# RWKV-style attention into a max-out MLP: token-major sums onto a bonus in PSUM, with every engine's order written out

## The chip, the core and the metric

The kernel runs on one core of one Trainium2 chip. The metric is the device time of one execution in microseconds (us); the value of a kernel is the median of its runs.

## The reference

For each batch and head a state of 48 x 48 is carried along 768 tokens; the output of a token sees the state before it and a bonus for the token itself. The result is then the input of a feed-forward block with the larger of two linear maps as its nonlinearity.

```python
B, H, S, D = 4, 8, 768, 48
for t in range(S):
    cur = einsum('bhd,bhe->bhde', u * k[t], v[t])
    y[t] = einsum('bhd,bhde->bhe', r[t], state + cur)
    state = w[t][..., None] * state + einsum('bhd,bhe->bhde', k[t], v[t])
x = y.transpose(0, 2, 1, 3).reshape(3072, 384)
out = maximum(x @ w1, x @ w2) @ w_out          # w1, w2: 384 x 1024, w_out: 1024 x 384
```

The kernel uses max(a, b) = (a + b + |a - b|) / 2: the hidden layer holds |x (w1 - w2)|, and x (w1 + w2) w_out / 2 is one product with a matrix wc that is made once.

## The kernel before

The tokens are cut into chunks of 128 (C), six for each sequence. A **unit** is one chunk of two sequences (NB = 2, called blocks b below), and there are twelve, chunk after chunk, the two pairs of sequences alternating. Units 10 and 11 are the last chunk and update no state.

For a unit, `attention` loads w, k, r and v, takes the logarithm of w (lw), sums it over the tokens of the chunk with a product by an upper triangle (`ex_p`, fp32, on PE), and takes exponentials: Aex (decay up to the token before), and Ainv (its inverse with the token itself) from incl = ex_p + lw. r and k are scaled by them into rp and kp, whose heads are padded to 64 columns. PE transposes both (`tp`), DVE copies them out (`rkT`), PE forms the scores of the eight heads (`mt_p`), and DVE masks them with the triangle (`MTm`). The output is summed in `y_p` **feature-major**: rows are features and columns tokens, three banks-worth of 128 features. Three products with the identity put in the bonus (vd, v times the row sums dg of r u k, made by DVE over L185, L186, L188 and L190); six put in the state's share; ten put in the values' share. Because a head's 48 features cross the borders of 128, `vz` and `sz` hold heads between zeros and are read through windows, so that a head can appear in two products. ACT copies `y_p` to xT, already in the shape that the feed-forward wants. `kv_p` collects k v for the state; DVE adds it to `sf` in two halves and scales it with Wx, the chunk's decay, which comes from the last row of incl through DRAM (`row`, `Wt`); POOL casts the state into `sz`.

`feed_forward` of the unit before follows: 24 products of the hidden layer (`g_p`) with ACT's absolute value (`gT`), then for each block three products with wc and eight with w_out (`o_p`), a copy (`osb`) and a store. `prep_weights` makes w1 - w2 (wd_sb), w1 + w2 (ws_sb), its transpose (wsT_sb) and wc after unit 0's attention.

Nothing in the code of before fixes the order on an engine: the framework's scheduler merges unit i's attention and unit i-1's feed-forward, within the limits of buffers. All loads and stores are issued from SP, one queue in order.

## Time and profile before

| what | us |
|---|---|
| median of 3 runs (193.05, 194.99, 195.09) | 194.99 |
| the profiled execution | 193.31 |
| its span, first to last instruction | 191.5 |
| busy in it: PE / DVE / ACT / POOL | 163.8 / 145.3 / 83.3 / 41.3 |
| idle of POOL before L248, waiting for DVE | 74.0 |
| idle of ACT before L228, waiting for PE | 43.9 |
| idle of DVE before L160, waiting for ACT's Aex | 21.3 |

PE is the tensor engine's products and PEld its weight loads, DVE the vector engine, ACT the scalar engine, POOL GpSimd and SP the queue that issues DMAs. A row of a group has line, engine, operation, written tile <- read tiles, shape and count, then busy time and the mean ns of one, then the idle time ahead of it and what ended that. A row of a timeline has start, length and what ran; "x8" joins eight instructions in a row.

### The profile page before, as it was taken

How to read it: one execution, taken by the hardware profiler on the slowest of the kernel's cores; microseconds unless marked ns; L12 is line 12 of the kernel's file. 1: busy time of each engine (PE TensorE's matmuls, PEld its weight loads, DVE VectorE, ACT ScalarE, POOL GpSimd, SP SyncE). 2: the span in 40 equal slices, each digit the busy share in tenths (PEclk: the TensorE clock that was granted, in tenths of full speed). 3: DMA queues.
4: the chain of work that ended last, by engine and by line, in shares of the span. 5: the costliest groups of instructions: out<-in, count | busy, mean ns of one | idle time of the engine just before them, and what ended most of it. 6: DMA issues, size and time to landing. Idle time of an engine off the chain costs nothing.

```text
span 191.5 us, 3963 instructions
## 1 busy us (share of the span) xinstructions
PE 163.8 (86%) x1624; PEld 111.7 (58%) x1624; DVE 145.3 (76%) x184; ACT 83.3 (43%) x158; POOL 41.3 (22%) x52
## 2 busy tenths in 40 slices
PE   0615875389999989999999999999999999999992
PEld 0203642236766667666766767667667666666761
DVE  0169998975747988999899799798997997937300
ACT  3120221313565365383573644734736357344351
POOL 8993020005021032041300310213103112100000
PEclk9999999999999999999999999999999999999999
DMA  6999998992029779498495894975948769110112
GB/s 140 219 331 382 196 281 221 199 166 47 3 92 233 132 154 169 106 215 147 98 234 88 184 182 92 236 138 122 213 84 203 133 135 195 38 44 5 41 41 82
DMA packets 112614, 28.82 MB, mean 150 GB/s; under 512 B 107594, under 2 KB 111818, under 8 KB 112596
## 3 DMA queue, kind: packets, MB, share of 16 engines
q1 hardware_dynamic: 112596, 28.58, 68.7%
q8 instruction: 12, 0.20, 0.4%
q14 instruction: 6, 0.05, 0.1%
HBM read 23.82 MB, written 4.75 MB: 149 GB/s over the span
## 4 chain that ended last, share of the span: by engine, by line
PE 48%; DVE 25%; issue 8%; ACT 8%; DMA 5%; SPq 3%; POOL 1%; ACTq 0%; DVEq 0%; POOLq 0%
PE o_p L272 13%; PE g_p L262 8%; PE y_p L225 7%; DVE MTm L210 6%; PE ex_p L158 5%; DVE sf L241 5%; DVE ku L186 4%; PE o_p L269 4%; ACT gT L265 4%; PE wc_p L120 3%; DMA u_b<-in_u_dram 3%; ACT Ainv L163 3%; SPq L130 3%; PE y_p L217 3%; PE mt_p L209 3%
## 5 line engine op out<-in xcount | busy, mean ns | idle before, releaser
L262 PE MATMUL g_p<-xT,wd_sb 128*128 128x256 bf16 x288 | 39.8, 272 | 1.1
L272 PE MATMUL o_p<-wo_sb,gT 128*128 128x384 bf16 x192 | 40.0, 327 | 0.0
L265 ACT ACTIVATE gT<-g_p 128x512 bf16<-128x512 f32 x48 | 27.9, 596 | 12.0 <-PE g_p L262 11.7
L248 POOL CAST sz<-sf 48x384 bf16<-48x384 f32 x20 | 16.1, 804 | 74.6 <-DVE sf L244 74.0
L210 DVE TENSOR_TENSOR MTm<-mt_p,triU 128x1024 bf16<-128x1024 f32 x24 | 29.3, 1221 | 3.5 <-PE mt_p L209 3.2
L262 PEld LDWEIGHTS <-wd_sb 128*128 128x128 bf16 x288 | 26.9, 97 | 8.0 <-issue 3.6
L228 ACT CAST xT<-y_p 128x384 bf16<-128x384 f32 x24 | 11.5, 479 | 44.0 <-PE y_p L225 43.9
L158 PE MATMUL ex_p<-lw,triU 128*128 128x384 f32 x48 | 23.1, 567 | 7.9 <-ACT lw L153 6.7
L160 DVE TENSOR_TENSOR incl<-ex_p,lw 128x384 f32<-128x384 f32 x24 | 13.3, 554 | 21.3 <-ACT Aex L159 21.3
L272 PEld LDWEIGHTS <-gT 128*128 128x128 bf16 x192 | 17.8, 98 | 10.0
L166 POOL CAST vz<-vt 128x768 bf16<-128x768 f32 x12 | 11.1, 928 | 47.0 <-DMA vt<-in_v_dram 38.2
L275 ACT COPY osb<-o_p 128x384 f32<-128x384 f32 x24 | 11.5, 479 | 19.6 <-PE o_p L272 19.5
L225 PEld LDWEIGHTS <-vz 128*128 128x128 bf16 x240 | 16.2, 102 | 6.5 <-issue 4.5
L225 PE MATMUL y_p<-MTm,vz 128*128 128x128 bf16 x240 | 18.4, 226 | 1.7 <-DVE MTm L210 1.7
L159 ACT ACTIVATE Aex<-ex_p 128x384 f32<-128x384 f32 x24 | 11.8, 491 | 16.4 <-PE ex_p L158 15.8
L269 PE MATMUL o_p<-wc_sb,xT 128*128 128x384 bf16 x72 | 17.3, 326 | 0.0
L203 DVE COPY rkT<-tp 128x1024 bf16<-128x1024 bf16 x24 | 16.4, 683 | 0.5 <-PE tp L200 0.5
L158 PEld LDWEIGHTS ex_p<-lw,triU 128*128 128x128 f32 x48 | 8.5, 210 | 10.6 <-issue 5.3
L165 DVE TENSOR_TENSOR kp<-kt,Ainv 128x768 bf16<-128x768 f32 x12 | 11.5, 957 | 3.5 <-ACT Ainv L163 3.5
L200 PE MATMUL tp<-ident,rp 128*128 128x128 bf16 x96 | 10.0, 231 | 4.1 <-DVE rp L164 4.1
L200 PE MATMUL tp<-ident,kp 128*128 128x128 bf16 x96 | 10.0, 231 | 3.1 <-DVE kp L165 3.1
L185 DVE TENSOR_TENSOR ku<-kt,u_b 128x768 f32<-128x768 f32 x12 | 11.8, 987 | 0.7 <-DMA u_b<-in_u_dram 0.7
(44 smaller groups left out, 202.7 us busy)
## 6 DMA issues: line engine op xcount, KB each, us to landing
wt<-in_w_dram SPq DMA_DIRECT2D x12, 384.0 KB
kt<-in_k_dram SPq DMA_DIRECT2D x12, 384.0 KB
rt<-in_r_dram SPq DMA_DIRECT2D x12, 384.0 KB
vt<-in_v_dram SPq DMA_DIRECT2D x12, 384.0 KB
out_dram<-osb SPq DMA_DIRECT2D x24, 192.0 KB
w1f<-in_moe_w_dram SPq DMA_DIRECT2D x3, 512.0 KB
w2f<-in_moe_w_dram SPq DMA_DIRECT2D x3, 512.0 KB
wof<-in_moe_w_out_dram SPq DMA_DIRECT2D x1, 1536.0 KB
```

What stands on the lines that cost most here:

```text
L158: nc.tensor.matmul(ex_p, triU, lw[:, b].rearrange("p h d -> p (h d)"))
L159: nc.scalar.activation(Aex[:, b].rearrange("p h d -> p (h d)"), ex_p, AF.Exp)
L160: nc.vector.tensor_add(incl[:, b].rearrange("p h d -> p (h d)"), ex_p, lw[:, b].rearrange("p h d -> p (h d)"))
L200: nc.tensor.transpose(tp[:, q, p, :], src[:, b, 2 * p:2 * p + 2, :].rearrange("p h d -> p (h d)"), ident)
L203: nc.vector.tensor_copy(rkT, tp)
L210: nc.vector.tensor_mul(MTm.rearrange("p a q c -> p (a q) c"), mt_p.rearrange("p a q c -> p (a q) c"), triU.unsqueeze(1).to_broadcast([C, H ...
L225: nc.tensor.matmul(y_p[:, j, :], vz[:, b, h * VS + o:h * VS + o + C], MTm[:, h % 2, h // 2, :], start=False, stop=(n == len(v_win) - 1), s ...
L248: nc.gpsimd.tensor_copy(S_z[bp][rows, :, C:].rearrange("p b (q e) -> p b q e", e=SS)[:, :, :, a * D:(a + 1) * D], S_f[bp][rows])
L262: nc.tensor.matmul(g_p[:, q, :], wd_sb[:, ko, fo * C:(fo + 1) * C], xT[:, ko].rearrange("p b c -> p (b c)"), start=(ko == 0), stop=(ko == ...
L265: nc.scalar.activation(gT[:, f2 * 2:f2 * 2 + 2, :], g_p, AF.Abs)
L269: nc.tensor.matmul(o_p, xT[:, ko, b, :], wc_sb[:, ko, :], start=(ko == 0), stop=False)
L272: nc.tensor.matmul(o_p, gT[:, fo, b * C:(b + 1) * C], wo_sb[:, fo, :], start=False, stop=(fo == FO - 1))
```

## The change

The new kernel does the same computation with the following differences.

- **Token-major sums.** `y_p` is one tile of 128 tokens x 384 features, kept for the whole kernel. DVE writes the bonus, v times dg, straight into it (`bonus_out`), and PE's products add onto that without a starting flag (`y_sum`): four state products of 96 columns and eight value products of 48 columns for each block, now with rkT and MTm as weights. One product with zeros at the start of the kernel prepares the bank. ACT copies the sum out as xs, PE transposes xs (`x_transposes`, three for each block) and DVE copies the result to xT (`x_out`). The windows and their zeros go; vb is a plain cast of v.
- **Engines.** ku = k u goes from DVE to POOL (`bonus_k`); the rkT copy of block 0 goes from DVE to ACT; the state's addition is one instruction of full height; kv products take the padded 64 columns; ws_sb goes to POOL and the scaling of w_out to ACT. Of ex_p, incl is now read ahead of Aex.
- **Order.** Everything stands in a manual schedule: each engine runs its instructions in the order of the code. `start` handles unit 0, its hidden layer, the weights and the first half of unit 1. Then `period(i, ...)` runs the attention of unit i, the first half (prefix sums, exponentials, scaling) of unit i+1, the feed-forward of unit i-1 and the loads and logarithm of unit i+2. In period 1 (`late`) the scaling and the bonus of unit 2 stand at the end, and no hidden layer is left to run.

The core of the diff (names as in the profile after; helpers that only wrap one instruction are left out):

```diff
+    y_p = ps.tile([C, HD], F32)
+    nc.tensor.matmul(y_p, ident, S_z[0].rearrange("p b q a d -> p (b q a d)")[:, 0:HD])
...
+    def excl(i, b):
+        ex_p = ps.tile([C, HD], F32, tag="ex")
+        nc.tensor.matmul(ex_p, triU, flat(st[i]["lw"][:, b]))
+        nc.vector.tensor_add(flat(st[i]["incl"][:, b]), ex_p, flat(st[i]["lw"][:, b]))
...
+    def bonus_k(i):
+        ku = work.tile([C, NB, HD], F32)
+        nc.gpsimd.tensor_mul(ku, tiles[i]["k"].rearrange("p b h d -> p b (h d)"),
+                             u_b.unsqueeze(1).to_broadcast([C, NB, HD]))
+    def bonus_out(i, b):
+        nc.vector.tensor_mul(y_p.rearrange("p (h d) -> p h d", d=D), tiles[i]["v"][:, b],
+                             st[i]["dg"][:, b * H:(b + 1) * H].to_broadcast([C, H, D]))
+    def y_sum(i, b):
+        c, bp = units[i]
+        if c > 0:
+            for p in range(PR):
+                nc.tensor.matmul(y_p[:, 2 * p * D:2 * (p + 1) * D], st[i]["rkT", b][:, 0, p, :],
+                                 S_z[bp][:, b, p].rearrange("p a d -> p (a d)"),
+                                 start=False, stop=False, skip_group_check=True)
+        for h in range(H):
+            nc.tensor.matmul(y_p[:, h * D:(h + 1) * D], st[i]["MTm", b][:, h % 2, h // 2, :],
+                             st[i]["vb"][:, b, h, :], start=False, stop=(h == H - 1),
+                             skip_group_check=True)
-            for j in range(KO):
-                nc.tensor.matmul(y_p[:, j, :], vd[:, b, j * C:(j + 1) * C], ident,
-                                 start=(j == 0), stop=False, skip_group_check=True)
-            if c > 0:
-                for p, j, o in s_win:
-                    nc.tensor.matmul(y_p[:, j, :], S_z[bp][:, b, p * SS + o:p * SS + o + C],
-                                     rkT[:, 0, p, :], start=False, stop=False,
-                                     skip_group_check=True)
-            for n, (h, j, o) in enumerate(v_win):
-                nc.tensor.matmul(y_p[:, j, :], vz[:, b, h * VS + o:h * VS + o + C],
-                                 MTm[:, h % 2, h // 2, :], start=False,
-                                 stop=(n == len(v_win) - 1), skip_group_check=True)
-            nc.scalar.copy(xT[:, :, b, :], y_p)
...
+    def period(i, j, f, more):
+        # A = unit i, P = unit j = i + 1, F = unit f = i - 1, M = unit more = i + 2
+        late = i == 1
+        tiles[M] = load(M)
+        bonus_out(A, 0); transposes(A, 0); transposes_out(A, 0)
+        if not late: bonus_r(P); bonus_sum(P); hidden(F, 0)
+        excl(P, 0); a_excl(P, 0); scores(A, 0); mask(A, 0)
+        transposes(A, 1); transposes_out(A, 1)
+        if not late: hidden(F, 1)
+        excl(P, 1); y_sum(A, 0); y_out(A, 0); a_excl(P, 1); scores(A, 1); mask(A, 1)
+        chunk_decay_row(P)
+        if not late: hidden(F, 2)
+        x_transposes(A, 0); a_inv(P)
+        if not late: hidden(F, 3)
+        bonus_out(A, 1); cast_v(P); y_sum(A, 1); y_out(A, 1); rows_out(F, 0, 0)
+        if not late: scaled_r(P)
+        log_w(M); bonus_k(M); x_transposes(A, 1); x_out(A); rows_out(F, 0, 1)
+        state_sum(A); chunk_decay_exp(A); store(F, 0); chunk_decay(P)
+        if not late: scaled_k(P)
+        state_out(A)
+        if late: scaled_r(P); scaled_k(P); bonus_r(P); bonus_sum(P)
+        rows_out(F, 1, 0); rows_out(F, 1, 1); store(F, 1)
```

(`period` is written here without its helper for missing units.) Three places of the engines' orders follow.

DVE in one steady unit of before, from the scaling of k on (rp and kp are the scaled r and k, ku, dg and vd the bonus, rkT and MTm the scores, sf the state, incl the prefix sum of the unit that follows):

```order
L165 TENSOR_TENSOR kp_85<-kt,Ainv 128x16x48
L186 TENSOR_TENSOR ku<-rt,ku 128x768
L203 COPY rkT<-tp 128x1024
L241 TENSOR_TENSOR sf_96<-kv_p,sf_96 48x384 x2
L210 TENSOR_TENSOR MTm<-mt_p,triU 128x1024
L203 COPY rkT<-tp 128x1024
L160 TENSOR_TENSOR incl<-ex_p,lw 128x384
L188 TENSOR_REDUCE dg<-ku 128x16
L210 TENSOR_TENSOR MTm<-mt_p,triU 128x1024
L190 TENSOR_TENSOR vd<-vt,dg 128x768
L244 TENSOR_TENSOR sf_96<-sf_96,Wx 128x384
L185 TENSOR_TENSOR ku<-kt,u_b 128x768
```

DVE in a steady period after, in the part from the start of the period to the second bonus:

```order
L229 TENSOR_TENSOR y_p<-vt,dg 128x384
L181 TENSOR_TENSOR ku<-rt,ku 128x768
L185 TENSOR_REDUCE dg<-ku 128x16
L133 TENSOR_TENSOR incl<-ex_p,lw 128x384
L222 TENSOR_TENSOR MTm<-mt_p,triU 128x1024
L208 COPY rkT<-tp 128x1024
L133 TENSOR_TENSOR incl<-ex_p,lw 128x384
L222 TENSOR_TENSOR MTm<-mt_p,triU 128x1024
L229 TENSOR_TENSOR y_p<-vt,dg 128x384
```

The bonus of the next unit (L181, L185) now stands ahead of this unit's first mask (L222), and each write of the bonus (L229) stands in the queue between masks; scaling and state come behind.

POOL of before, between two casts of the state (sz) in the steady part, then POOL after:

```order
L248 CAST sz_97<-sf_96 48x2x4x48 x2
L166 CAST vz_86<-vt 128x2x8x48
L248 CAST sz_101<-sf_100 48x2x4x48 x2
L166 CAST vz_92<-vt 128x2x8x48
L248 CAST sz_97<-sf_96 48x2x4x48 x2
```

```order
L284 CAST sz_97<-sf_96 48x8x48 x2
L190 CAST vb<-vt 128x768
L175 TENSOR_TENSOR ku<-kt,u_b 128x768
L284 CAST sz_93<-sf_92 48x8x48 x2
L190 CAST vb<-vt 128x768
```

POOL has one more instruction in each unit, the product ku with two inputs, between the cast of v and the casts of the state.

SP, the queue of all DMAs, before (the loads of a unit are wt, kt, rt, vt; row and Wt carry the chunk's decay through DRAM; osb is a block of the result):

```order
L173 DMA row<-incl 1x768
L130 DMA wt<-in_w_dram 128x16x48
L175 DMA Wt_104<-row 48x8x1 x2
L130 DMA kt<-in_k_dram 128x16x48
L277 DMA out_dram<-osb 128x384
L130 DMA rt<-in_r_dram 128x16x48
L277 DMA out_dram<-osb 128x384
L130 DMA vt<-in_v_dram 128x16x48
```

SP after, one period:

```order
L111 DMA wt<-in_w_dram 128x16x48
L111 DMA kt<-in_k_dram 128x16x48
L111 DMA rt<-in_r_dram 128x16x48
L111 DMA vt<-in_v_dram 128x16x48
L143 DMA row<-incl 1x768
L316 DMA out_dram<-osb 128x384
L150 DMA Wt_102<-row 48x8x1 x2
L316 DMA out_dram<-osb 128x384
```

The four loads, which were spread over the unit between row, Wt and the stores, stand together at the head of the period, and both Wt transfers and the second store stand behind the row.

More of the change, by code (lines that the diff above doesn't have):

```diff
@@ new lines, in transposes_out, with scores @@
+    def transposes_out(i, b):
+        rkT = work.tile([C, 2, PR, C], BF16, bufs=3)
+        if b == 0:
+            nc.scalar.copy(rkT, st[i].pop(("tp", b)))
+        else:
+            nc.vector.tensor_copy(rkT, st[i].pop(("tp", b)))
+        st[i]["rkT", b] = rkT
+    def scores(i, b):
+        rkT = st[i]["rkT", b]
+        mt_p = ps.tile([C, 2, PR, C], F32, tag="mt")
+        for p in range(PR):
+            for a in range(2):
+                rows = slice(a * DP, a * DP + D)
+                nc.tensor.matmul(mt_p[:, a, p, :], rkT[rows, 1, p, :], rkT[rows, 0, p, :])
+        st[i]["mt", b] = mt_p
@@ L279 @@
[L279 to L295 removed]
+                    h = 2 * p + a
@@ new lines, in store, with prep_sums, prep_transposes @@
+    def store(i, b):
+        c, bp = units[i]
+        osb = mlp.tile([C, HD], F32, bufs=4)
+        nc.scalar.copy(osb, st[i].pop(("o", b)))
+        row = (bp * NB + b) * S + c * C
+        nc.sync.dma_start(out=out[row:row + C, :], in_=osb)
+    tiles = {}
+    n = len(units)
+    def prep_sums(ko):
+        nc.gpsimd.tensor_add(ws_sb[:, ko, :], w1f[:, ko, :], w2f[:, ko, :])
+        nc.vector.tensor_sub(wd_sb[:, ko, :], w1f[:, ko, :], w2f[:, ko, :])
+    def prep_transposes(ko):
+        tp = ps.tile([C, FO, C], BF16, tag="mlp", bufs=2)
+        for fo in range(FO):
+            nc.tensor.transpose(tp[:, fo, :], ws_sb[:, ko, fo * C:(fo + 1) * C], ident)
+        nc.vector.tensor_copy(wsT_sb[:, :, ko * C:(ko + 1) * C], tp)
@@ L297 @@
+    with tc.manual_schedule():
+        start()
+        for i in range(1, n + 1):
+            period(i if i < n else None, i + 1 if i + 1 < n else None, i - 1,
+                   i + 2 if i + 2 < n else None)
     ps.release()
```

418 lines of the change are left out of this document (262 added, 156 removed).

## The prediction

> **What bounds the kernel now.** I read the page's head and its chain first, then busy time by stage, then PE's and DVE's rows in one steady stretch.
>
> ```profile
> span 191.5 us, 3963 instructions
> PE 163.8 (86%) x1624; PEld 111.7 (58%) x1624; DVE 145.3 (76%) x184; ACT 83.3 (43%) x158; POOL 41.3 (22%) x52
> PE 48%; DVE 25%; issue 8%; ACT 8%; DMA 5%; SPq 3%; POOL 1%; ACTq 0%; DVEq 0%; POOLq 0%
> ```
>
> The chain changes between PE and DVE; neither is alone the bound. The stages (columns: busy us of PE, PEld, DVE, ACT, POOL) show where:
>
> ```profile
> 12.00:31.00 19.00, 11.27 (x100) 8.12 (x98) 18.27 (x20) 2.19 (x4) 5.10 (x7) 1.00 1.06 309
> 31.00:46.00 15.00, 10.33 (x62) 5.03 (x63) 11.23 (x15) 3.55 (x7) 2.43 (x3) 1.00 0.85 149
> 96.10:108.70 12.60, 12.31 (x138) 8.71 (x136) 11.29 (x16) 6.64 (x13) 2.43 (x3) 1.00 0.80 162
> ```
>
> The reader is to see a start of 46 us in which PE is poorly filled and DVE is full, and then stretches of 12.6 us, one for each unit, in which PE shows 12.3 and DVE 11.3 busy. A busy PE overstates itself, since the matmuls overlap, so I take distances between starts (columns: start, length, what):
>
> ```profile
> 98.79 0.38 PE L236 MATMUL kv_p<-vz,kp 128*48 128x48 bf16 x16
> 99.11 0.72 PE L262 MATMUL g_p<-xT,wd_sb 128*128 128x256 bf16 x5
> ...
> 100.61 0.39 PE L200 MATMUL tp<-ident,rp 128*128 128x128 bf16 x4
> ...
> 101.06 0.49 PE L269 MATMUL o_p<-wc_sb,xT 128*128 128x384 bf16 x2
> ...
> 102.24 0.72 PE L225 MATMUL y_p<-MTm,vz 128*128 128x128 bf16 x10 [0.20 <-DVE MTm L210]
> 102.89 0.40 PE L209 MATMUL mt_p<-rkT 48*128 48x128 bf16 x8
> 103.22 0.34 PE L272 MATMUL o_p<-wo_sb,gT 128*128 128x384 bf16 x1
> ...
> 103.69 0.50 PE L221 MATMUL y_p<-rkT,sz 128*128 128x128 bf16 x6
> 104.02 0.81 PE L272 MATMUL o_p<-wo_sb,gT 128*128 128x384 bf16 x4
> ...
> 107.02 0.81 PE L158 MATMUL ex_p<-lw,triU 128*128 128x384 f32 x2
> 107.66 0.33 PE L217 MATMUL y_p<-ident,vd 128*128 128x128 bf16 x3
> ```
>
> So 16 kv products take 0.32 (20 ns each), 8 transposes 0.45, 10 value products 0.65, 8 scores 0.33 (41 ns each), 6 state products 0.33, one fp32 prefix sum 0.64. The tail gives the feed-forward:
>
> ```profile
> 181.33 3.09 PE L262 MATMUL g_p<-xT,wd_sb 128*128 128x256 bf16 x24
> 184.40 0.65 PE L269 MATMUL o_p<-wc_sb,xT 128*128 128x384 bf16 x3
> 184.88 1.46 PE L272 MATMUL o_p<-wo_sb,gT 128*128 128x384 bf16 x8
> 186.18 0.65 PE L269 MATMUL o_p<-wc_sb,xT 128*128 128x384 bf16 x3
> ```
>
> The hidden layer is 3.07, one block of output rows 1.78, of which eight products are 1.30. A unit's work on PE before is thus 1.28 (prefix) + 0.90 (transposes) + 0.66 (scores) + 0.34 (bonus, 6) + 0.66 (state) + 1.25 (values) + 0.32 (kv) + 3.07 + 3.56 = 12.0 of 12.6 us: a twentieth is waiting.
>
> **What the change removes and adds in a unit.** On PE go 6 bonus products, 12 state and 20 value products; there come 8 state products of 96 columns, 16 value products of 48 columns and 6 transposes of x. No row has 48 moving columns against a weight of 128 columns. The kv row has the 48 columns (20 ns), the state row full size (55 ns); the score row, whose weights are 128 columns wide, lies between at 41 ns. I take 41: 24 products cost 0.98, and the x transposes 0.34, for 2.25 before. PE's new sum is 1.28 + 0.90 + 0.66 + 0.98 + 0.34 + 0.32 + 3.07 + 3.56 = **11.1 us**; by the two ends 10.6 and 11.4.
>
> ```profile
> L210 DVE TENSOR_TENSOR MTm<-mt_p,triU 128x1024 bf16<-128x1024 f32 x2 | 2.4, 1220 | 0.0
> L160 DVE TENSOR_TENSOR incl<-ex_p,lw 128x384 f32<-128x384 f32 x3 | 1.7, 554 | 1.9 <-ACT Aex L159 1.9
> L203 DVE COPY rkT<-tp 128x1024 bf16<-128x1024 bf16 x2 | 1.4, 682 | 0.0
> L185 DVE TENSOR_TENSOR ku<-kt,u_b 128x768 f32<-128x768 f32 x1 | 1.0, 954 | 0.0
> L188 DVE TENSOR_REDUCE dg<-ku 128x16 f32<-128x768 f32 x1 | 0.9, 942 | 0.0
> L244 DVE TENSOR_TENSOR sf<-sf,Wx 128x384 f32<-128x384 f32 x1 | 0.6, 551 | 0.0
> ```
>
> DVE loses L185 to POOL (0.95), vd of the same width (0.95), one rkT copy to ACT (0.68) and one of the two half-height sf additions (0.55): 3.1 us. It gains two bonus writes into y_p, 384 wide as L244 (1.1), and the copy of xT, 768 wide, between 0.55 and 0.68 (0.6): 1.7 us. From 11.3 busy it falls to 9.9. The wait of L160 for Aex goes too, because the addition now stands ahead of the exponential; DVE's waits then come from PE.
>
> ```profile
> L265 ACT ACTIVATE gT<-g_p 128x512 bf16<-128x512 f32 x4 | 2.3, 596 | 1.2 <-PE g_p L262 1.2
> L228 ACT CAST xT<-y_p 128x384 bf16<-128x384 f32 x2 | 1.0, 480 | 3.2 <-PE y_p L225 3.2
> ```
>
> 128 more columns cost ACT 0.116, so the 1024-column rkT copy is 0.60 + 4 x 0.116 = 1.06. ACT grows from 6.6 to about 7.7 a unit: cover enough, but the copy now stands between the transposes and the scores of a unit, with the previous block's osb ahead of it and the first gT behind it.
>
> POOL gains ku. No row shows POOL with two inputs. Its casts do, with one:
>
> ```profile
> 26.21 1.22 DVE L109 TENSOR_TENSOR wd_sb<-w1f,w2f 128x1024 bf16<-128x1024 f32 x1
> 26.88 1.23 POOL L166 CAST vz<-vt 128x768 bf16<-128x768 f32 x1 [11.01 <-DMA vt<-in_v_dram]
> 27.34 1.84 DVE L110 TENSOR_TENSOR ws_sb<-w1f,w2f 128x1024 bf16<-128x1024 f32 x1
> ...
> L166 POOL CAST vz<-vt x12: 823/827/1249, 14.7 to 162.6; 128x768 bf16<-128x768 f32 x12
> ...
> L248 POOL CAST sz<-sf x20: 500/802/1121, 43.1 to 158.5; 48x384 bf16<-48x384 f32 x20
> ```
>
> The 768-wide cast is 0.83 undisturbed, so ku is 0.83 to 1.65 (twice); I take 1.65, since it reads two tensors. By the Trainium skill, "GPSIMD Engine Reference", section 3.1, a two-input operation runs at about 2.6 cycles per element at 1.2 GHz, an estimate of 1.66 us; the sum would not move.
>
> The first three rows show more: the cast lasted 1.23 beside L109 (two SBUF inputs, ending at 27.43), and L110, at 27.34, lasted 1.84 instead of 1.22, to 29.18, which is 1.1 after the cast's end. Each waited for the other. The Trainium skill, "SBUF — State Buffer", section "SBUF: two separate sides", says that a GpSimd instruction and a VectorE one with two SBUF inputs hold a shared port pair exclusively, whole instruction by whole instruction; the trace agrees. This speaks against the change: POOL's 2.4 us of work a unit becomes 0.83 + 1.65 + 1.0 = 3.5, and bonus_out, bonus_r, scaled_r, scaled_k and the sf product all read two SBUF tensors.
>
> **One period, from the first transpose at 0.** The sf product of the unit before ends at -0.3, bonus_out ends at 0.25. The sz cast that asked meanwhile goes first (0.50), then bonus_r, bonus_sum, incl and the mask, 0.95 + 0.94 + 0.55 + 1.22, less some 0.08 for each overlap, end at 4.2. PE runs transposes 0.45, hidden 0.77, prefix 0.64 to 1.86 (rkT is out of ACT at 1.75), then scores, transposes, hidden, prefix to 4.05, and waits until 4.2 for y_sum. That takes 0.49; the second scores wait 0.1 for rkT and end at 5.15. Two hidden quarters and x transposes go to 6.9; the second mask (1.22) and bonus_out behind it end at 7.0. Then y_sum 0.49, output rows 3.56, x transposes 0.17, kv 0.32: **11.6 us**, with 0.5 of waiting. The end of DVE's queue (scaled_k at about 10.6) is ahead of the next transposes.
>
> **The queues passed.** SP now issues four loads at once, then row, a store, two Wt, a store.
>
> ```profile
> 96.37 0.45 SPq L173 DMA_DIRECT2D row<-incl  x1
> ...
> 99.24 0.91 SPq L175 DMA_DIRECT2D Wt<-row  x2
> ```
>
> Wt waits 2.9 for row to land; behind the four loads row lands when vt does. The DMA engines are busy 0.80 x 12.6 = 10 us a period, loads some 8 of it, so loads, row, Wt issue (0.91) and store give a loop of about 11.4, just inside the period. Behind the Wt stand the second store and the next loads; they are used half a period or more after landing, which hides 0.3 a period of slippage.
>
> **Start.**
>
> ```profile
> 12.49 0.96 DVE L185 TENSOR_TENSOR ku<-kt,u_b 128x768 f32<-128x768 f32 x1 [0.72 <-DMA u_b<-in_u_dram]
> 13.37 0.95 DVE L165 TENSOR_TENSOR kp<-kt,Ainv 128x768 bf16<-128x768 f32 x1
> ...
> 38.98 6.57 PE L120 MATMUL wc_p<-wo_sb,wsT_sb 128*128 128x384 bf16 x24 [1.48 <-DVE wo_sb L111]
> 45.48 0.40 PE L209 MATMUL mt_p<-rkT 48*128 48x128 bf16 x8
> ```
>
> kp no longer stands behind the ku that waits for u_b: it starts at 11.8, not 13.4. But POOL's ku (from 12.75, after kp), cast and three ws additions of 2.2 (1.65 x 1024 / 768) end at 22 to 23.5 with the alternation above. The preparation on DVE (three wd, three wsT, xT, 6 us) lets the first hidden quarter begin at 29.5. Until 45.5 PE is slow: 24 wc products take 6.57 where eight of that width take 1.30 later. Behind 29.5 stand 3.07 + 1.28 + 3.9 of full-speed work and some 2.7 of waits, 40.5; all at the slow speed it would be 44.6. PE is filled from 29.5 on, so I take **41** for the first transposes of unit 1, with unit 0's hidden layer already done.
>
> **The sum.** 41; the first period, without hidden layer, lasts 11.8 because rp and kp of unit 2 stand behind the state; in the second DVE is 1.8 late (bonus_r, bonus_sum moved behind kp), 13.0; seven periods 81.2; the tenth, without kv products, 11.2; the eleventh, without prefix sums as well, 10.4; the last hidden layer and rows 6.6; osb and store 3.4 as before. Together 178.6, against 191.5. The profiled execution was 193.31, 1.81 around its span, which gives 180.4; the median of the runs, 194.99, lies 0.9% above that execution, so I say **181**.
>
> **Rivals.** (1) Small products at 20 ns and waits hidden: 10.8 a period, start 39: 178.6 - 2 - 8 x 0.7 = 171, time 173. Against it: DVE's chain to the masks does not shrink with PE. (2) The port pair is held where it hurts once: ku on POOL starts just ahead of bonus_out for block 1 and delays y_sum by 1 us a period: 178.6 + 9, time 189. For it: kt lands near the middle of the period. Against: kt is behind wt in the queue, so likelier at 7 than at 6.3. (3) The DMA loop sets the period, 12.3: time 186. (4) **Slower**: POOL goes first every time, both sz casts and the v cast ahead of bonus_r (1.4 more) and ku ahead of bonus_out (1.6): 14.6 a period, 178.6 + 27, time 207. It decides from 1.6 us a period of added wait on. For it: L110 above was held 0.62 by one cast. Against: DVE's next operation mostly starts before POOL has its semaphore. Between (2) and (4), at 1.5 a period, the time would be as before.
>
> **Chances.** Forecast 0.48 (176 to 185), rival 1 0.13, rival 2 0.16, rival 3 0.05, same 0.07, slower 0.11. A measurement of this kernel can tell about 1%. Faster 0.82, same 0.07, slower 0.11. The range goes from the fast rival to the held port, 172 to 190.
>
> **What would show it.** In the profile after: transposes of successive units 11.6 apart; y_sum products 30 to 45 ns apart; waits of y_sum for MTm and y_p of 0.2 to 0.3; ku on POOL 1.65; unit 1's transposes at 41. It is wrong if DVE's two-input rows show lengths well over 0.95 and PE waits over 1 us for y_p, or if lw waits for wt.

## The result, and the profile after

| | us |
|---|---|
| after, median of 4 runs (180.67, 183.35, 184.89, 185.99) | 184.12 |
| before, median of 4 runs beside them | 194.36 |
| ratio, 95% interval | 0.937 (0.922 to 0.953) |
| profiled execution of after, its span | 183.35, 181.6 |

The kernel became faster by about 6%; 181 was forecast, with a range of 172 to 190. The medians are of all runs, but the ratios, here and below, leave out runs more than 1.5% above the fastest of their kernel, in after 184.89 and 185.99, so 0.937 is not 184.12 over 194.36. The page's head, busy times and chain of after:

```profile
span 181.6 us, 3831 instructions
PE 151.1 (83%) x1537; PEld 101.8 (56%) x1537; DVE 130.1 (72%) x172; ACT 95.0 (52%) x171; POOL 65.7 (36%) x63
PEclk9999999999699699999999999999999999999999
PE 55%; DVE 25%; issue 6%; ACT 4%; DMA 4%; SPq 3%; POOL 1%; ACTq 0%; DVEq 0%; POOLq 0%
```

PE and DVE still take turns in the chain. New is the line of the granted clock (PEclk, in tenths of full speed): it falls to 0.6 in two slices, of 4.5 us each, at about 47 and 61 us. Its first figures say nothing: the trace has no record of the clock ahead of 33.33 us, and the view shows 1.00 there. Busy time by stage (columns: length; PE, PEld, DVE, ACT, POOL; granted clock, DMA share, GB/s), cut at the first transposes of a unit:

```profile
12.00:31.00 19.00, 9.80 (x101) 7.82 (x102) 14.96 (x16) 5.40 (x6) 12.62 (x6) 1.00 1.03 314
31.00:39.85 8.85, 8.50 (x46) 4.88 (x46) 5.14 (x7) 4.81 (x9) 0.82 (x1) 1.00 0.95 181
39.85:53.42 13.57, 10.54 (x98) 5.88 (x96) 8.08 (x13) 6.47 (x13) 6.46 (x6) 0.87 0.69 132
53.42:69.57 16.15, 12.95 (x128) 8.54 (x129) 13.61 (x18) 7.09 (x14) 4.76 (x5) 0.89 0.59 124
69.57:150.08 80.51, 78.81 (x899) 54.71 (x896) 71.71 (x99) 51.89 (x98) 33.43 (x29) 1.00 0.85 173
```

PE is nearly filled from 31 us on, and seven steady periods take 80.51, or 11.50 each, where seven units of before took 87.69. Between start and steady part stand periods 1 and 2, much longer than the rest and at a clock of 0.87 and 0.89. Unit 1's scores begin at 42.33 instead of 45.48, unit 2's first transposes at 53.42 instead of 59.66 and unit 3's at 69.57 instead of 72.79: of the 6.2 us won by then, period 2 gives back 3.0. One steady period on PE, in part:

```profile
92.64 0.39 PE L198 MATMUL tp<-ident,rp 128*128 128x128 bf16 x4
...
93.09 0.82 PE L295 MATMUL g_p<-xT,wd_sb 128*128 128x256 bf16 x6
93.75 0.81 PE L132 MATMUL ex_p<-lw,triU 128*128 128x384 f32 x2
...
98.47 0.82 PE L295 MATMUL g_p<-xT,wd_sb 128*128 128x256 bf16 x6
99.50 0.33 PE L236 MATMUL y_p<-sz,rkT 128*128 128x96 bf16 x4 [0.21 <-DVE y_p L229]
99.67 0.36 PE L240 MATMUL y_p<-vb,MTm 128*128 128x48 bf16 x8
99.87 0.65 PE L304 MATMUL o_p<-wc_sb,xT 128*128 128x384 bf16 x3
...
104.15 0.39 PE L198 MATMUL tp<-ident,rp 128*128 128x128 bf16 x4
```

From start to start four state products take 0.17 (43 ns each), eight value products 0.20 (25 ns each) and a hidden quarter 0.66; the quarter ahead of y_sum's second block takes 1.03, with 0.37 of waiting for the bonus in it. The groups of POOL, DVE and ACT that the prediction priced (busy, mean ns of one, then idle time ahead):

```profile
L175 POOL TENSOR_TENSOR ku<-kt,u_b 128x768 f32<-128x768 f32 x12 | 24.4, 2031 | 48.2 <-DMA kt<-in_k_dram 40.7
L181 DVE TENSOR_TENSOR ku<-rt,ku 128x768 f32<-128x768 f32 x12 | 14.5, 1204 | 2.0 <-POOL ku L175 2.0
L229 DVE TENSOR_TENSOR y_p<-vt,dg 128x384 f32<-128x384 f32 x24 | 15.2, 635 | 0.1
L206 ACT COPY rkT<-tp 128x1024 bf16<-128x1024 bf16 x12 | 12.1, 1012 | 3.2 <-PE tp L198 3.2
```

The means lie above the undisturbed 0.95 of L181 and 0.56 of L229; the rows of single instructions below show where they were stretched.

**Where periods 1 and 2 went.** The end of period 1 and the first half of period 2 on DVE, and the PE instruction that waited:

```profile
52.41 0.95 DVE L168 TENSOR_TENSOR rp<-rt,Aex 128x768 bf16<-128x768 f32 x1
53.28 1.26 DVE L171 TENSOR_TENSOR kp<-kt,Ainv 128x768 bf16<-128x768 f32 x1
54.46 1.25 DVE L181 TENSOR_TENSOR ku<-rt,ku 128x768 f32<-128x768 f32 x1
55.75 0.95 DVE L185 TENSOR_REDUCE dg<-ku 128x16 f32<-128x768 f32 x1
56.74 0.57 DVE L229 TENSOR_TENSOR y_p<-vt,dg 128x384 f32<-128x384 f32 x1
57.22 0.95 DVE L181 TENSOR_TENSOR ku<-rt,ku 128x768 f32<-128x768 f32 x1
58.20 0.95 DVE L185 TENSOR_REDUCE dg<-ku 128x16 f32<-128x768 f32 x1
59.07 0.55 DVE L133 TENSOR_TENSOR incl<-ex_p,lw 128x384 f32<-128x384 f32 x1
60.26 1.31 PE L132 MATMUL ex_p<-lw,triU 128*128 128x384 f32 x2 [2.42 <-ACT Aex L137]
```

Four instructions of unit 2's preparation (rp, kp, ku, dg) stand behind the state of unit 1, and DVE works them off while PE has already begun period 2. The addition incl, which with Aex behind it frees the only buffer of `ex_p`, comes at 59.07; PE has nothing else in its order and stops for 2.42 us. What follows in the granted clock, over two stretches of 3.42 us, the first behind period 1's stop of 1.38 us (PE waiting for L229, the bonus of block 1) and the second behind this one:

```profile
46.98:50.40 3.42, 3.42 (x21) 1.86 (x21) 0.44 (x1) 1.32 (x3) 1.53 (x1) 0.50 0.80 145
60.64:64.06 3.42, 3.42 (x30) 2.20 (x29) 2.54 (x5) 0.92 (x3) 1.18 (x1) 0.50 0.65 128
```

Both have a granted clock of exactly half. 3.42 us at half speed do 1.71 us of work, so each costs up to 1.7 us, if PE is the bound in them. The same lengths stand in the start, where no clock was recorded: a hidden quarter at 29.49 lasts 1.44 us and the prefix products behind it 1.49, against 0.82 and 0.81 above.

### The profile page after: what moved, and what is told of

Same layout as the page of the kernel before. It is cut to its first block, busy times and chain, and to the rows that moved or that the text cites. A ratio compares the mean times of both kernels' runs of the same rounds, so it can differ in the third digit from the quotient of the medians.

```text
span 181.6 us, 3831 instructions
## 1 busy us (share of the span) xinstructions
PE 151.1 (83%) x1537; PEld 101.8 (56%) x1537; DVE 130.1 (72%) x172; ACT 95.0 (52%) x171; POOL 65.7 (36%) x63
## 4 chain that ended last, share of the span: by engine, by line
PE 55%; DVE 25%; issue 6%; ACT 4%; DMA 4%; SPq 3%; POOL 1%; ACTq 0%; DVEq 0%; POOLq 0%
PE o_p L308 14%; PE ex_p L132 8%; PE g_p L295 8%; DVE MTm L222 8%; PE o_p L304 6%; DVE y_p L229 5%; PE mt_p L217 4%; DMA u_b<-in_u_dram 4%; DVE ku L181 3%; PE tp L198 3%; SPq L111 3%; PE y_p L236 3%; PE y_p L240 3%; PE wc_p L334 2%; PE kv_p L268 2%
## 5 line engine op out<-in xcount | busy, mean ns | idle before, releaser
L175 POOL TENSOR_TENSOR ku<-kt,u_b 128x768 f32<-128x768 f32 x12 | 24.4, 2031 | 48.2 <-DMA kt<-in_k_dram 40.7
L308 PE MATMUL o_p<-wo_sb,gT 128*128 128x384 bf16 x192 | 37.9, 332 | 0.0
L222 DVE TENSOR_TENSOR MTm<-mt_p,triU 128x1024 bf16<-128x1024 f32 x24 | 29.3, 1220 | 4.8 <-PE mt_p L217 4.3
L132 PE MATMUL ex_p<-lw,triU 128*128 128x384 f32 x48 | 23.3, 571 | 10.2 <-ACT lw L122 6.4
L284 POOL CAST sz<-sf 48x384 bf16<-48x384 f32 x20 | 18.0, 898 | 35.8 <-DVE sf L279 32.8
L314 ACT COPY osb<-o_p 128x384 f32<-128x384 f32 x24 | 11.5, 479 | 30.6 <-PE o_p L308 30.6
L246 ACT CAST xs<-y_p 128x384 bf16<-128x384 f32 x24 | 11.5, 480 | 19.3 <-PE y_p L240 12.9
L137 ACT ACTIVATE Aex<-ex_p 128x384 f32<-128x384 f32 x24 | 11.8, 493 | 16.6 <-DVE incl L133 16.6
L257 DVE COPY xT<-xt_p 128x768 bf16<-128x768 bf16 x12 | 6.7, 557 | 15.0 <-PE xt_p L253 15.0
L181 DVE TENSOR_TENSOR ku<-rt,ku 128x768 f32<-128x768 f32 x12 | 14.5, 1204 | 2.0 <-POOL ku L175 2.0
L240 PE MATMUL y_p<-vb,MTm 128*128 128x48 bf16 x192 | 9.2, 188 | 7.5 <-DVE MTm L222 4.0
L229 DVE TENSOR_TENSOR y_p<-vt,dg 128x384 f32<-128x384 f32 x24 | 15.2, 635 | 0.1
L206 ACT COPY rkT<-tp 128x1024 bf16<-128x1024 bf16 x12 | 12.1, 1012 | 3.2 <-PE tp L198 3.2
L240 PEld LDWEIGHTS <-MTm 128*128 128x128 bf16 x192 | 7.6, 99 | 8.5 <-DVE MTm L222 6.8
```

Source lines behind the costliest of these rows:

```text
L132: nc.tensor.matmul(ex_p, triU, flat(st[i]["lw"][:, b]))
L175: nc.gpsimd.tensor_mul(ku, tiles[i]["k"].rearrange("p b h d -> p b (h d)"), u_b.unsqueeze(1).to_broadcast([C, NB, HD]))
L181: nc.vector.tensor_mul(ku, tiles[i]["r"].rearrange("p b h d -> p b (h d)"), ku)
L222: nc.vector.tensor_mul(MTm.rearrange("p a q c -> p (a q) c"), st[i].pop(("mt", b)).rearrange("p a q c -> p (a q) c"), triU.unsqueeze(1).to ...
L229: nc.vector.tensor_mul(y_p.rearrange("p (h d) -> p h d", d=D), tiles[i]["v"][:, b], st[i]["dg"][:, b * H:(b + 1) * H].to_broadcast([C, H, D]))
L240: nc.tensor.matmul(y_p[:, h * D:(h + 1) * D], st[i]["MTm", b][:, h % 2, h // 2, :], st[i]["vb"][:, b, h, :], start=False, stop=(h == H - 1 ...
```

## The experiments

Names of units and periods are those of the code. "Period 1" is the distance from unit 1's first transposes to unit 2's, and so on. Each ratio is to runs of before on the same chip, with its 95% interval; the span is that of the profiled execution.

| run | what | median us | ratio | span | periods 1 / 2 / steady |
|---|---|---|---|---|---|
| after | | 184.12 | 0.937 (0.922, 0.953) | 181.6 | 13.57 / 16.15 / 11.50 |
| e1 | unit 2's preparation earlier | 179.10 | 0.930 (0.926, 0.935) | 177.3 | 13.76 / 11.32 / 11.5 |
| e2 | after, scheduler's order | 188.93 | 0.985 (0.977, 0.994) | 187.1 | steady 12.9 |
| e3 | ku on DVE | 183.07 | 0.949 (0.942, 0.956) | 180.4 | 12.46 / 16.17 / 11.5 |
| e4 | PE refilled in period 2 | 182.55 | see text | 182.5 | 15.72 / 14.89 / 11.5 |
| e5 | before with token-major sums | 199.15 | 1.036 (1.030, 1.041) | 196.9 | steady 13.5 |
| e6 | e1, hidden layer of unit 0 in period 1 | 177.86 | 0.926 (0.921, 0.931) | 175.8 | 14.02 / 11.57 / 11.5 |
| e7 | e1, sz casts on ACT | 184.52 | 0.961 (0.954, 0.967) | 182.3 | steady 11.9 |
| e9 | e1, ku on DVE | 180.13 | 0.933 (0.926, 0.940) | 178.4 | 13.69 / 11.57 / 11.5 |
| e10 | e6, unit 2's bonus late | 179.14 | 0.928 (0.923, 0.932) | 179.2 | 12.17 / 16.45 / 11.5 |
| e11 | e10, one hidden quarter back | 178.71 | 0.927 (0.922, 0.931) | 176.7 | 11.53 / 15.70 / 11.5 |
| e12 | e11, unit 2's bonus early | 175.32 | 0.910 (0.905, 0.915) | 172.6 | 11.53 / 12.60 / 11.5 |

### The backlog (e1) and the stop (e4)

e1 takes the backlog away: unit 2's rp, bonus and kp leave their place behind the state.

```diff
-        if not late: scaled_r(P)
+        scaled_r(P)
+        if late: bonus_r(P); bonus_sum(P)
         log_w(M); bonus_k(M); x_transposes(A, 1); x_out(A); rows_out(F, 0, 1)
...
-        if not late: scaled_k(P)
+        scaled_k(P)
         state_out(A)
-        if late: scaled_r(P); scaled_k(P); bonus_r(P); bonus_sum(P)
```

> Only the late block of period 1 is changed: scaled_r, bonus_r and bonus_sum of unit 2 stand behind the second bonus of unit 1, where DVE idles 3.1 us (46.86 to 49.96), and scaled_k ahead of the state. Theory: DVE's backlog sets periods 1 and 2 (29.7 us together where 24.8 were forecast), by the PE gap of 2.4 us at 57.8 to 60.3 and by the half clock that follows it (0.50 from 61 to 64). Expected: both periods together 24 to 25, no gap over 1 us and clock 1.0 in period 2, span 176 to 177.5. Rival: the clock falls anyway, because period 1 has no hidden layer to fill PE; then only the gap goes, span 179 or more.

Periods 1 and 2 of e1:

```profile
40.10:53.86 13.76, 10.39 (x98) 5.89 (x97) 11.80 (x17) 6.21 (x12) 5.96 (x6) 0.88 0.70 130
53.86:65.18 11.32, 11.11 (x130) 7.81 (x129) 10.02 (x15) 7.42 (x14) 4.24 (x5) 1.00 0.87 176
```

Period 2 falls from 16.15 to 11.32 at full clock, and the runs, which lay 5.3 us apart, now lie between 178.88 and 179.46. Period 1 stays long, with a stop of 2.00 us and a half-speed stretch of its own; both periods together take 25.08, just over the 24 to 25 expected. So the place of four instructions of unit 2, with the stop and the half speed behind it, accounts for the whole excess of period 2.

e4 leaves the backlog and refills the stop: the second hidden quarter of unit 1 is computed four times in period 2 (the same products again).

```diff
-        for q in range(2):
+        for q in [0, 1] * times:
...
-        hidden(F, 1)
+        hidden(F, 1, 4 if i == 2 else 1)
```

> In period 2 the second quarter of the hidden layer is computed four times over (each starts its sums anew, so the result is the same): some 2 us of PE work in the gap of 2.4 us. Theory (the half clock is a consequence of the gap): clock 1.0 through period 2, period 2 shorter by 1.5 to 2 us, span 179.5 to 180. Rival (the clock falls for another reason, or the products of that stretch are hidden): span unchanged, 181 to 182.

In the profiled execution period 2 is 14.89 at a clock of 1.00, 1.26 less than after although PE does more. This agrees with the theory that the half speed there follows from the stop, but it is one execution, the longest of the four. The other traces bear it out: in all four with that stop in period 2 (after, e3, e10 and e11, 2.38 to 2.97 us) half speed begins between 0.42 us ahead of its end and 0.37 behind it, and none of the six variants of after without it (e1, e4, e6, e7, e9, e12) has half speed in period 2. The span, 182.5, met neither expectation, because period 1 became longer, 15.72, in the same execution (the four times lie between 178.75 and 184.22, so no ratio is given); 6.83 us of it ran at half speed, in after 3.42. The longer stop is in two rows of it, and one that waited:

```profile
46.40 1.80 POOL L175 TENSOR_TENSOR ku<-kt,u_b 128x768 f32<-128x768 f32 x1 [0.96 <-DMA kt<-in_k_dram]
46.46 2.16 DVE L229 TENSOR_TENSOR y_p<-vt,dg 128x384 f32<-128x384 f32 x1
48.68 0.48 PE L240 MATMUL y_p<-vb,MTm 128*128 128x48 bf16 x8 [2.98 <-DVE y_p L229]
```

POOL's ku began 0.06 us ahead of DVE's bonus, and the bonus, 0.56 long in after, took 2.16: it ended 0.42 after ku did. In e1 ku began at 45.49 and the bonus, from 46.54, took 1.18; in after ku began at 46.70, behind the bonus. ku starts when kt lands, so a few tenths of a us in a transfer decide over 1.6 us of PE (the stop is 2.98 here and 1.38 in after).

### Is ku on POOL worth it? (e3, e9)

Both put ku back on DVE: e3 in the changed kernel, e9 in e1.

```diff
-        nc.gpsimd.tensor_mul(ku, ...
+        nc.vector.tensor_mul(ku, ...
```

> ku = k u back on DVE, at the same place of the order. Theory: DVE idles 1.07 us there (waiting for the transposes of x), which holds 0.87 us of ku, and POOL no longer holds DVE; steady periods 11.4 to 11.7, as after. Rival: DVE is close enough to the bound that 0.9 us comes through, 12.4 a period, time 191 or more.

> e1 (span 177.3, 179.1 us) with ku = k*u_b on VectorE instead of GpSimd. Theory 1 (GpSimd's ku holds VectorE's two-input product into y_p in period 1: it took 0.56, 1.18 and 2.16 us in three kernels, ending each time with a ku of 1.81 us on GpSimd that had started before it; in the steady periods TensorE sets the pace and the place of ku does not matter): the product takes 0.55, TensorE's gap before y_p of chunk 1 falls from 2.00 to 1.4 or less, steady periods 11.5, time 178 to 179.3. Rival (0.95 us more on VectorE in each period is more than the 0.3 that its hold costs): steady periods 11.7 or more, 181 to 183.

The steady period is the same, 11.50 in after, 11.5 in e3 and 11.51 in e9, with DVE then taking 11.1 of it. DVE's wait for the transposes of x, which was 1.06 in after, shrinks in e3:

```profile
111.67 0.56 DVE L257 COPY xT<-xt_p 128x768 bf16<-128x768 bf16 x1 [0.20 <-PE xt_p L253]
```

So the move to POOL gave DVE slack that nothing used; the 0.95 us a unit are not part of the 6%. In e9's period 1 the bonus takes 0.56 and the stop before y_p is 1.38, as expected without a neighbour on POOL. The period is 13.69 all the same, at a clock of 1.00: kv then waits 1.73 us for xT, which stands behind unit 2's bonus on DVE. And e9 missed its time, 180.13 against at most 179.3: with ku of unit 0, which waits for u_b, ahead of kp on DVE again, unit 0's transposes begin at 14.55 instead of 11.91, its kv products at 30.04 instead of 28.41, and unit 1's transposes at 41.00 instead of 40.10. That the move to POOL is worth this 0.9 us in the start is not shown: e3, with the same start and its kv products at 30.02, reaches unit 1 at 39.73, since its first hidden quarter and prefix products last 0.81 each, in e9 1.44 and 1.48. The same start thus came out 1.27 us apart, more than the 0.9, and the intervals of e1's and e9's ratios overlap.

e3 also shows the clock's other side. Its stop in period 1 is the same 1.38 us, and the 3.41 us ahead of its end are filled as in after. The stretch ahead of the end of the stop in after, and then the one in e3 with what followed:

```profile
43.57:46.98 3.41, 1.86 (x24) 1.14 (x25) 3.25 (x5) 1.70 (x3) 2.00 (x3) 1.00 1.14 227
```

```profile
43.79:47.20 3.41, 1.86 (x22) 1.14 (x23) 3.38 (x6) 1.70 (x3) 0.21 (x1) 1.00 1.29 228
47.20:50.61 3.41, 3.41 (x43) 2.21 (x43) 1.91 (x3) 1.80 (x4) 0.00 (x0) 1.00 0.55 89
```

PE was busy 1.86 us in both, and yet after ran at half speed behind it and e3 at full; period 1 was 13.57 in the one and 12.46 in the other. That fits a clock set from fixed stretches of time that know nothing of the kernel: the same stop lies in one stretch or across two. In the clock records of all traces the times between two changes are whole multiples of 3.41 us (3.41, 6.83, 10.24, 13.65, 20.48, 23.89, 30.72). Counted so, the stretch from 43.57 in after holds the stop with 1.86 us of PE work, while in e3 the stretches begin at 42.23 and 45.65 and hold 2.61 and 2.03. How much work is enough is not shown: e9 kept full speed behind a stretch with 1.68 us (50.41 to 53.82). The Trainium skill, "TensorE: Matmul & The Clock Gate", section "Part 1: The HAM clock gate (the "warmup" mystery)", gives a free-running window of about 3.4 us, and the halved stretches of 3.42 agree; it asks for an idle window, and here PE had 1.86 and 0.99 us of work in those that were followed by half speed, so "idle" is not to be taken as empty.

### Filling period 1 (e6, e10, e11, e12)

e6 moves the four hidden quarters of unit 0 from the start into period 1, where every later period has its quarters.

```diff
-            hidden(0, q)
...
-        if not late: bonus_r(P); bonus_sum(P); hidden(F, 0)
+        if not late: bonus_r(P); bonus_sum(P)
+        hidden(F, 0)
...
-        if not late: hidden(F, 1)
+        hidden(F, 1)
```

(and likewise for the other two quarters)

> On top of the run that moves unit 2's preparation forward (e1, span 177.3, period 1 13.76): the four quarters of unit 0's hidden layer no longer stand in the start but in period 1, where every later period has them. Theory 1 (period 1 is long because TensorE has 8 us of full-speed work in 11.5, stops for 2.0 us before y_p of chunk 1 and then runs at half clock): with the quarters there the gap closes below 1 us, the clock stays over 0.9 from 44 to 54, period 1 takes 11.3 to 12.2 instead of 13.76, and the start ends 1 to 3 us earlier (hidden x24 took 6.1 us there at a slow clock, beside other work): span 173 to 176. Rival (TensorE is then cold in the start and the wc sums, 24 matmuls in 4.06 us, take up to 8.1 at half clock): first transposes of unit 1 still at 40 or later, span 175 to 178. Rival 2 (VectorE's chain, not TensorE's clock, sets period 1): period 1 stays at 13 or more, span 177 or more.

The start ends 2.0 us earlier, at 38.13, the stop before y_p is 0.21 instead of 2.00, and the clock stays at 1.00. But period 1 is not shorter, 14.02. So rival 2 is right on the length and on DVE's chain as its reason, though the span, 175.8, is theory 1's; what stretched the chain it did not foresee:

```profile
45.13 2.54 POOL L175 TENSOR_TENSOR ku<-kt,u_b 128x768 f32<-128x768 f32 x1 [1.56 <-DMA kt<-in_k_dram]
45.91 2.57 DVE L181 TENSOR_TENSOR ku<-rt,ku 128x768 f32<-128x768 f32 x1
49.39 0.55 DVE L257 COPY xT<-xt_p 128x768 bf16<-128x768 bf16 x1
49.99 0.43 PE L268 MATMUL kv_p<-vb,kp 128*64 128x48 bf16 x16 [2.48 <-DVE xT L257]
```

Now DVE's bonus product is the one that meets POOL's ku, and lasts 2.57 instead of 0.95; dg and xT stand behind it, and PE waits 2.48 us for xT before kv. No half speed follows this stop.

e10 puts only bonus_r and bonus_sum of unit 2 back to the end of period 1; e11 returns one hidden quarter to the start.

```diff
-        if late: bonus_r(P); bonus_sum(P)
         log_w(M); bonus_k(M); x_transposes(A, 1); x_out(A); rows_out(F, 0, 1)
...
         state_out(A)
+        if late: bonus_r(P); bonus_sum(P)
```

> Unit 0's hidden layer in period 1 as in e6, unit 2's rp and kp where every later unit has them, and only its ku and dg (bonus_r, bonus_sum) at the end of period 1, behind the state. Theory 1 (period 1 of e6 was 14.0 because its xT copy stood behind a bonus product that GpSimd's ku held for 2.57 us, which made TensorE wait 2.48 before kv): xT follows rp, kv waits below 0.7, period 1 is 11.5 to 12.3, all clocks stay at 1.0, span 173.3 to 174.3, time 175 to 176. Rival (the bonus moved behind the state now stands ahead of the bonus product of unit 2 and brings back the backlog of the changed kernel's period 2): period 2 is 13 or more instead of 11.57, span 176 or more.

> As e10, with the first of unit 0's four hidden quarters back in the start, where TensorE stood idle for 1.17 us before the second prefix product. Theory 1 (that quarter fits into the idle time, and period 1 has less to do on TensorE): start ends 0 to 0.5 later, period 1 shorter by 0.3 to 0.7, span 0 to 0.6 below e10. Rival (VectorE, 13.2 of 14.0 us busy in e6's period 1, sets period 1): period 1 as in e10, span the same or 0.5 above.

Period 1 does what theory 1 said, 12.17 in e10 and 11.53 in e11 (the quarter that went back shortens the start as well, to 37.67). e11's span is 2.5 us below e10's, where at most 0.6 was expected; e10's profiled execution, the longest of its six, ran at half speed for 6.83 us of period 2 and e11's for 3.41, and the medians are only 0.4 apart. The rival is right on period 2: two late instructions of 0.95 us bring all of the backlog back. e11's two periods, and the stop in the second:

```profile
37.67:49.20 11.53, 10.53 (x115) 6.97 (x114) 9.96 (x15) 7.70 (x15) 5.60 (x5) 1.00 0.96 173
49.20:64.90 15.70, 12.73 (x131) 8.54 (x129) 13.20 (x18) 7.31 (x14) 4.39 (x5) 0.89 0.62 128
55.62 1.65 PE L132 MATMUL ex_p<-lw,triU 128*128 128x384 f32 x2 [2.97 <-ACT Aex L137]
```

e12 combines what worked: xT ahead of the sum, both bonus instructions ahead of the state.

```diff
         scaled_r(P)
+        if late: bonus_r(P)
         log_w(M); bonus_k(M); x_transposes(A, 1); x_out(A)
+        if late: bonus_sum(P)
         rows_out(F, 0, 1)
...
         state_out(A)
-        if late: bonus_r(P); bonus_sum(P)
```

> As e11 (span 176.7, period 1 11.53, period 2 15.70), with unit 2's bonus product directly behind its rp and its sum directly behind xT, both ahead of the state, so that nothing of unit 2's preparation is left for period 2. Theory 1 (the two late instructions of 0.95 us each, and nothing else, make period 2's stop of 2.4 to 3.0 us and its half clock): period 2 is 11.3 to 11.6, period 1 stays at 11.5 to 12.5, no stop of TensorE above 1 us and no granted clock under 0.95 from 40 us on, span 172.5 to 174, time 174.3 to 175.8. Rival 1 (GpSimd's ku of unit 3 holds the bonus product for up to 1.6 us, as in e6, and xT and kv behind it): period 1 13 to 14, span 174.5 to 175.8. Rival 2 (period 2 is long for another reason, such as the loads): period 2 stays above 13, span 175 or more.

```profile
36.43:47.96 11.53, 10.54 (x115) 6.97 (x114) 10.93 (x16) 7.70 (x15) 5.82 (x5) 1.00 0.96 180
47.96:60.56 12.60, 11.30 (x130) 7.81 (x128) 11.19 (x17) 7.31 (x14) 5.35 (x5) 1.00 0.79 162
52.51 0.91 PE L132 MATMUL ex_p<-lw,triU 128*128 128x384 f32 x2 [1.10 <-ACT Aex L137]
```

At 175.32 us, ratio 0.910 (0.905 to 0.915), it is faster than both kernels. The time and the span, 172.6, are those of theory 1, with the clock at 1.00 from its first record, at 27.38, on; period 2 is not, 12.60 against 11.3 to 11.6. DVE enters it late: its first bonus begins 0.73 behind unit 2's first transposes (48.69 and 47.96), in a steady period 0.30 ahead of them (92.34 and 92.64 in after), and PE's stop of 1.10 for Aex is about that difference. 1.2 us of the profiled span come from the start, which has the code of e11: there the first hidden quarter and the first prefix products took 1.44 and 1.36, the lengths of half speed, here 0.81 each (the first record of the clock stands at 31.59 there and at 27.38 here). Whether the runs of e12, 174.33 to 177.33, differ by this is not shown.

### The order and the sums, each alone (e2, e5)

e2 runs after's instructions, on the same engines, without the manual schedule, so that the scheduler orders them. e5 is the kernel before with the token-major sums alone; its engines, its start and the scheduler's order are those of before.

```diff
-    with tc.manual_schedule():
+    if True:
         start()
```

```diff
-            y_p = ps.tile([C, KO, C], F32, tag="y")
-            (three bonus, six state, ten value products, copy to xT)
+            nc.vector.tensor_mul(y_p..., t["v"][:, b], dg...)
+            (four state, eight value products onto y_p, copy to xs, three transposes)
```

> The instructions of after, without the manual schedule: the framework's scheduler orders them. Theory 1 (the work counts): with 11.1 us of PE work and 10 of DVE work a unit any sound order gives periods of 11.5 to 11.8, time within 2% of after. Theory 2 (the order counts): the merged order of before returns its waits, 12.2 or more a unit, and the start is about as long as before's 45 us; time 188 to 193.

> The kernel before with the token-major sums alone: bonus multiplied straight into the PSUM tile y_p, the old state's and MTm's small products added to it, copied to xs, three transposes to channel-major. The scheduler keeps the order, ku stays on VectorE, the start is the one of before. Theory 1 (the order gives most of the gain, the sums little by themselves; the run with the changed instructions in the scheduler's order gave 0.985 of before): ratio 0.97 to 1.00, a period of 12.4 to 13.2 us, TensorE waiting for VectorE's bonus product or MTm. Rival (the sums take their 0.9 us of TensorE off every period and that is the gain whatever the order): ratio 0.93 to 0.95, period 11.5 to 11.8.

The steady stretches, seven units of before, six of e5 and six of e2, and of e2 the two largest waits that DVE has:

```profile
72.79:160.48 87.69, 85.64 (x946) 60.17 (x944) 79.73 (x105) 45.90 (x90) 18.05 (x21) 1.00 0.77 156
```

```profile
84.82:165.70 80.88, 71.42 (x766) 45.55 (x765) 73.90 (x102) 40.29 (x80) 14.28 (x17) 1.00 0.72 146
```

```profile
76.55:153.97 77.42, 72.03 (x783) 46.44 (x782) 59.86 (x85) 45.81 (x87) 21.90 (x24) 1.00 0.78 157
L133 DVE TENSOR_TENSOR incl<-ex_p,lw 128x384 f32<-128x384 f32 x24 | 13.3, 554 | 19.8 <-PE ex_p L132 19.8
L222 DVE TENSOR_TENSOR MTm<-mt_p,triU 128x1024 bf16<-128x1024 f32 x24 | 29.3, 1219 | 13.2 <-PE mt_p L217 13.2
```

A unit takes 12.53 in before, 13.48 in e5, 12.90 in e2 and 11.50 in after. Fewer and smaller products make the scheduler's steady period longer, not shorter: PE is busy 85.64 of 87.69 in before and only 71.42 of 80.88 in e5. The sums are now a chain from DVE's bonus over PE, ACT, PE and DVE (y_p, xs, xt_p, xT), where before they ended with ACT's copy. In e5 PE waits 4.8 us each for rp, for kp and for xs over the whole run; how much of that the longer chain makes was not separated. e5 is outside both of its expectations, slower by 3.6%, and the loss lies in the steady part: its unit 4 begins at 84.82, before's at 84.74, its unit 10 at 165.70 and before's at 160.48. Its low clock in the start (0.70 over 34 to 50 us) cost nothing that the runs show: a run with a granted clock of 0.998 over the whole took 198.64, the profiled one with 0.965 198.70. e2's whole gain of 1.5%, too small to be called faster, lies ahead of the steady part (unit 3's transposes at 63.48, in before at 72.79). So in the steady part the sums and the new engines alone are a loss, and the written order on top of them is worth 1.4 us a period. Whether an order written out for before's products would gain as much was not tried. By distances between starts, with a hidden layer at 4 x 0.66 = 2.64, PE's work in a unit of before is about 11.6 of 12.53 (an estimate), so at most 0.9 us stood open to an order alone.

### The casts of the state (e7)

e7 is e1 with the sz casts on ACT, so that they no longer meet DVE's bonus product.

```diff
-            nc.gpsimd.tensor_copy(S_z[bp][rows, :, :, a, :], S_f[bp][rows])
+            nc.scalar.copy(S_z[bp][rows, :, :, a, :], S_f[bp][rows])
```

> e1 with the two casts sz (48 x 384) on ScalarE instead of GpSimd, so that they no longer meet VectorE's product for the bonus. Theory 1 (TensorE is busy 11.1 of 11.5 us, so the 0.3 us that VectorE's L181 loses beside a cast lies in VectorE's slack): L181 0.95 instead of 1.25, steady periods 11.4 to 11.5, time 178.5 to 179.6. Rival (the hold is part of what stands between 11.1 and 11.5): periods 11.2 to 11.3, 176.5 to 178. Rival 2 (two casts of about 0.5 us on ScalarE stand ahead of rkT or gT and make TensorE wait): periods 11.7 or more, 181 or more.

L181 falls to 0.95, and the kernel is slower than e1 by 5 us, 11.9 a period: rival 2. (The first bonus of a unit, L229, grew from 0.56 to 1.18 or 1.19 in most periods, where the cast vb on POOL met it.) ACT is not too full; the casts wait at the head of its queue.

```profile
102.70 1.03 ACT L284 CAST sz<-sf 48x384 bf16<-48x384 f32 x2 [1.46 <-DVE sf L279]
103.76 0.48 ACT L314 COPY osb<-o_p 128x384 f32<-128x384 f32 x1
104.14 1.02 ACT L206 COPY rkT<-tp 128x1024 bf16<-128x1024 bf16 x1
105.21 0.40 PE L217 MATMUL mt_p<-rkT 48*128 48x128 bf16 x8 [0.41 <-ACT rkT L206]
```

(three rows of ACT, then one of PE.) 1.46 us of waiting for sf and 1.03 of casts stand ahead of osb and rkT, and PE's scores wait for rkT, 6.3 us in the whole run.

## Why the prediction was right, point by point

| step | forecast | after |
|---|---|---|
| transposes of unit 1 | 41 | 39.85 |
| period 1 | 11.8 | 13.57 |
| period 2 | 13.0 | 16.15 |
| seven periods | 81.2 | 80.51 |
| periods 10 and 11 | 21.6 | 21.3 |
| last hidden layer, rows, osb and store | 10.0 | 10.2 |
| span | 178.6 | 181.6 |

- **The steady period was right, 11.50 for 11.6**, and with it the direction; that it came so near is partly luck. The 24 small products were taken at 41 ns and cost 43 and 25, together 0.74 instead of 0.98. The hidden layer was taken at 3.07, from the tail, where its quarters stand apart; in the steady part a quarter takes 0.66, all four 2.64. With these two the work is about 10.4 instead of 11.1, and so 1.1 of the 11.50 is waiting where 0.5 was taken: 0.37 before y_sum, 0.16 for Aex ahead of the second prefix products (from 95.28 to 96.10 a quarter takes 0.82), the rest in smaller parts. No lw but the very first waits for wt, so the loop of SP did not set the period; that its loads follow each other by 11.4 (105.27 and 116.64) is no test of the 11.4 worked out, since they come once a period.
- **The place of the miss was named, its size was not.** "In the second DVE is 1.8 late (bonus_r, bonus_sum moved behind kp), 13.0": the backlog is there, in those instructions, and e1, e6 and e9, with period 2 at 11.32 to 11.57, show that without them it is as short as a steady one (e12 keeps 12.60). But the 1.8 was charged as if PE lost only what DVE was late; rp and kp stood behind it too and were stretched, the stop was 2.42, and behind it came 3.42 us at half clock that the sum had no term for. After minus e1 is 4.8 us in this period, against the 1.4 that were charged (13.0 over 11.6).
- **Period 1**, 11.8 forecast: without hidden quarters PE has nothing to run while DVE makes the second mask and bonus, a stop of 1.38, and again half clock. e3, with the same stop and full clock, gives 12.46; so of the 1.8 us missed about 1.1 are the clock, if the place of ku makes no other difference there. PE waiting over 1 us for y_p was one of the signs of being wrong; it came here, once, but not from a held port: L229 lasted 0.56.
- **Rival 2 did not happen in the profiled execution, but came near.** In period 1 ku starts at 46.70, 0.40 behind the bonus; in e4, the same code up to there, it starts 0.06 ahead and holds the bonus by 1.6 us. In the steady period ku starts at 99.63 and the bonus at 98.89: 0.7 us is the margin. The prediction had argued by kt's landing, which was right. **Rival 4** fell: one sz cast stretches L181 to 1.26, 0.3 a period. That this lies in DVE's slack was not shown by itself, but e3's 0.95 us more of DVE work left the period at 11.5.
- **ku on POOL** took 1.80 to 1.81 undisturbed (1.65 taken), the three ws additions 2.34 to 3.05, with DVE beside them (2.2 taken); neither was on the path, and the first hidden quarter began at 29.49 as forecast.
- The median lies 3.1 above the forecast, since the terms of the two periods are 4.9 too small and the start and the steady part 1.8 too large. The step from 180.4 to 181 is a slip as well: 0.9% more is 182.0. The runs of after differ by their clock, 0.987 at 180.67 and 0.971 at 185.99. An estimate from these: about 4.7 us at half speed in the one and 10.7 in the other, against 6.8 in the profiled execution (0.981). Where these stretches lay, and whether the phase of the clock's windows or kt's landing decided, is not shown.

## What to carry to other kernels

Follow the first two or three periods of a written pipeline instruction by instruction: what a special case leaves behind the state there stops the engine that has run out of work, and on PE a stop of 1.4 to 3.0 us can be followed by 3.4 us at half speed, which cost up to 1.7 us more. A sum with less work for the busiest engine gained nothing in the steady part here until the order around it was written anew, so price a new data path together with its order. On an in-order engine look at what an instruction waits for before you move it there: the cast that is free on an idle engine held up everything behind it on a half-busy one.
